# The split of the first columns of x on VectorE and ScalarE, and the later columns' GpSimd operations spread over the feed-forward's blocks

## Chip, cores and metric

The kernel runs on one core of a Trainium2 chip. The metric is device time in microseconds (us) per execution, and the number compared is the median of several. TensorE (PE) does matrix products, VectorE (DVE) and GpSimd (POOL) elementwise work, ScalarE (ACT) elementwise functions, and SyncE's queue (SP) issues all DMAs. Every engine takes its instructions in the order in which they are queued on it.

## What is computed

Attention with queries pooled in pairs, followed by a feed-forward network with g = h - tanh(h). The attention's output, rearranged to 4608 tokens of 512 columns, is the feed-forward's x.

```python
def _attn_ref(q, k, v):                      # (8, 8, 1152, 64) each
    q_pool = q.reshape(B, H, S // 2, 2, D).mean(axis=3)
    scores = (1.0 / np.sqrt(D)) * np.matmul(q_pool, k.transpose(0, 1, 3, 2))
    scores = scores - np.max(scores, axis=-1, keepdims=True)
    attn = np.exp(scores)
    attn = attn / (np.sum(attn, axis=-1, keepdims=True) + 1e-09)
    return np.matmul(attn, v)

def _moe_ref(x, w_in, w_out):                # (4608, 512), (512, 2048), (2048, 512)
    h = x @ w_in
    g = h - np.tanh(h)
    return g @ w_out
```

## The kernel before

**Precision.** Every operand of a large matrix product is split in a high part, rounded to the fp32r format, and a low part, the remainder; a product is the sum of high x high, high x low and low x high. So x exists as `x_h` and `x_l`, each for four feature tiles of 128 (the index `hp`, 0 to 3).

**Attention** runs over 32 pairs of heads (`n_pair`), each in 36 units (`U`). A unit is one key tile of one head and half of the queries: two score matmuls into `ps_s`, one exponential on ScalarE into `p_f`. Each six units are a group, for which POOL adds up the exponentials (`z_part`, two additions), and whose value matmuls (`pv`) come some units later. `z_sums` turns the partial sums into row sums on TensorE, `z_out` copies these to `z_s` on ScalarE, and `store` writes the unnormalised output `o_s` to `x_dram` and the sums to `z_dram`. For each batch the sums are read back (`rec`), inverted and written to `r_dram`, so that the division takes place when the feed-forward loads x.

The order of all this is written out by hand: `add(u, f)` puts a piece of work at unit u, after that unit's score matmuls and exponential, and `add(..., at=first)` ahead of them. `end` is 1152, the unit after the last exponential. All engine handles of this stage (`pe`, `act`, `dve`, `pool`, `sp`) are `InOrder`: what is issued through them stays in this order on its engine. All their instructions appear in the profile under line 37, the helper's.

**x.** `load_x` (lines 96 to 121) prepares up to 512 columns (tokens) of x. For each feature tile, `fetch` issues one DMA for the unnormalised x into `x_f` and, for each of two heads and each batch touched, one for the inverted sums into `x_r`; `work` then runs three POOL operations on 128 partitions: the product `x_f` times `x_r` (the division), the high part (times 1 plus 0, rounded on output), and the low part by subtraction. The pool `xt` has one buffer of `x_f` and one of `x_r`, so that the next feature tile's transfer can start only when these are free again. The first columns, chunk 0, are prepared at the end of attention (lines 416 to 421), feature tile j's fetch at unit end - 14 + 8j and its work 5 units later. Six blocks of weights (four of `wi`, two of `wo`) are loaded at units end - 17 to end - 12 into `spare`, buffers of attention that are free by then (lines 424 to 430).

**Feed-forward.** There are ten chunks of columns: eight of 512 and two of 256. For each chunk the loop over `fc` runs through 16 blocks of the hidden dimension: `hidden` makes twelve matmuls into `ps_h` (line 521), an elementwise chain on ScalarE and VectorE (527 to 537), the high part `g_hi` on ScalarE (538) and the low part `g_lo` on POOL (539); `second`, two blocks behind (`LAG`), multiplies by `wo` (line 546). The other weight blocks are loaded at its beginning (lines 509 to 515) into a pool that takes the place of attention's buffers. The x of chunk ci + 1 is prepared in chunk ci: `load_x` in the program at fc = 2, and at fc = 2 to 5 one feature tile each, fetch and three POOL operations together (lines 571 to 576); `x_h` and `x_l` have two pairs of buffers. `issue_after` keeps this work behind the last SP and POOL instruction of attention and does nothing else. In this stage no `InOrder` is used: a scheduler with its own estimate of times picks, for each engine, among what it takes to be ready, the earlier in the program first, and so sets the order on the engine's queue when the kernel is built.

Of the kernel before, what the change touches and what calls it, by code (L numbers as in the profile page):

```python
# [8 lines left out]
F32 = mybir.dt.float32  # L9
F32R = mybir.dt.float32r  # L10
I32 = mybir.dt.int32
AF = mybir.ActivationFunctionType
ALU = mybir.AluOpType
# [30 lines left out]
def kernel(  # L44
# [17 lines left out]
    nc = tc.nc  # L62
    P = 128
    B, NP, _, _, SQ = q.shape
# [28 lines left out]
    wi_dram = dram.tile([NF, P, 2, NP, P], F32, name="wi_dram")  # L93
    wo_dram = dram.tile([NF, P, 2, DM], F32, name="wo_dram")

    def load_x(tiles, sp, pool, t0, n):

        x_h, x_l = (t.rearrange("p (c n) -> p c n", c=NP) for t in tiles())

        t = {}  # L100

        def fetch(hp):
            x = xt.tile([P, 512], F32, name="x_f")
            r = xt.tile([P, 512], F32, name="x_r")
            t[hp] = x, r
            sp.dma_start(x[:, 0:n], x_dram[hp, :, t0:t0 + n])
            c = t0
            while c < t0 + n:
                b, c1 = divmod(c, SQ)
                m = min(SQ - c1, t0 + n - c)  # L110
                for h in range(2):
                    sp.dma_start(r[h * 64:h * 64 + 64, c - t0:c - t0 + m],
                                 r_dram[b, h, hp:hp + 1, c1:c1 + m].broadcast_to([64, m]))
                c += m

        def work(hp):
            x, r = t[hp]
            pool.tensor_tensor(x[:, 0:n], x[:, 0:n], r[:, 0:n], op=ALU.mult)  # L118
            pool.tensor_scalar(x_h[:, hp, 0:n], x[:, 0:n], 1.0, 0.0, op0=ALU.mult, op1=ALU.add)  # L119
            pool.tensor_tensor(x_l[:, hp, 0:n], x[:, 0:n], x_h[:, hp, 0:n].bitcast(F32), op=ALU.subtract)  # L120
        return x_h, x_l, [(lambda hp=hp: fetch(hp), lambda hp=hp: work(hp)) for hp in range(NP)]

    xp = [ctx.enter_context(tc.tile_pool(name="xp0", bufs=2))]

    def x_tile(i):
        return xp[i].tile([P, NP * 512], F32R, name="x")

    op0 = ctx.enter_context(tc.tile_pool(name="op0", bufs=1))
    xt = ctx.enter_context(tc.tile_pool(name="xt", bufs=1))
    rec = ctx.enter_context(tc.tile_pool(name="rec", bufs=2))  # L130
    chunks = [(t, min(512, NTOK - t)) for t in range(0, NTOK, 512)]
    t, n = chunks.pop()
# [4 lines left out]
    with ExitStack() as actx:  # L137
# [3 lines left out]
        op = actx.enter_context(tc.tile_pool(name="op", bufs=1))  # L141
# [7 lines left out]
        pe, act, dve, pool, sp = (InOrder(tc, e) for e in (nc.tensor, nc.scalar, nc.vector, nc.gpsimd, nc.sync))  # L149
# [23 lines left out]
        at, first = {}, {}  # L173
        end = n_pair * U

        def add(u, f, *args, at=at):
            at.setdefault(u, []).append(lambda: f(*args))
# [29 lines left out]
        def hi_part(pi, c0, c1):  # L207
            w = pairs[pi]
            act.activation(w.hi[:, c0:c1], w.kq[:, c0:c1], AF.Copy)

        def lo_part(pi, c0, c1):
            w = pairs[pi]
            dve.tensor_tensor(w.lo[:, c0:c1], w.kq[:, c0:c1], w.hi[:, c0:c1].bitcast(F32), op=ALU.subtract)
# [143 lines left out]
        def reciprocals(eng, b, t):  # L357

            eng.scalar_tensor_tensor(t[:, 0], t[:, 0], 1e-9, t[:, 1], op0=ALU.add, op1=ALU.add)
            eng.reciprocal(t[:, 0], t[:, 0])  # L360

        def spread(dma, b, t):
            dma.dma_start(r_dram[b].rearrange("h a (x n) -> (h a x) n", n=SQ * NP * 2 // P), t[:, 0])
# [51 lines left out]

        tot = []
        x0 = []
        add(end - 15, lambda: x0.extend(load_x(lambda: (x_tile(0), x_tile(0)), sp, pool, *chunks[0])))
        for j in range(NP):
            for i in range(2):  # L420
                add(end - 14 + 8 * j + 5 * i, lambda i=i, j=j: x0[2][j][i]())


        spare = [t.rearrange("p h n -> p (h n)")[:, i:i + 1024] for t in tt[0] for i in range(0, 3072, 1024)]
# [1 line left out]
        for i, (t, w_dram) in enumerate(((wi, wi_dram), (wi, wi_dram), (wi, wi_dram), (wo, wo_dram), (wi, wi_dram), (wo, wo_dram))):  # L426
            f = len(t)
# [47 lines left out]
        for u in range(end + 60):  # L475
            run(u, first)
            if u < end:
                pi, r = divmod(u, U)
                half, r = divmod(r, U // 2)
                g, r = divmod(r, G)  # L480
                h, j = divmod(r, 3)
# [14 lines left out]
            n, slot = divmod(u - 2 * G + 1, G)  # L496
# [20 lines left out]
    def hidden(x_h, x_l, n, fc):  # L517
        h = ps_h.tile([P, 512], F32, name="ps_h")[:, 0:n]
        mm = [(w, x, c) for w, x in ((0, x_h), (0, x_l), (1, x_h)) for c in range(NP)]
        for j, (w, x, c) in enumerate(mm):  # L520
            nc.tensor.matmul(h, wi[fc][:, w, c], x[:, c, 0:n], start=(j == 0), stop=(j == len(mm) - 1))  # L521

        def t(name, dtype=F32, bufs=2):
            return gp.tile([P, 512], dtype, name=name, bufs=bufs)[:, 0:n]
        u, th, s1, s2, w, m = t("g_u"), t("g_t"), t("g_s1"), t("g_s2"), t("g_w"), t("g_m", bufs=1)
        g_h, g_l = t("g_hi", F32R, LAG + 1), t("g_lo", F32R, LAG + 1)
        nc.scalar.activation(u, h, AF.Square)  # L527
        nc.scalar.activation(th, h, AF.Tanh)
        nc.scalar.activation(s2, u, AF.Square, bias=pc[:, 1:2])  # L529
        nc.scalar.activation(s1, u, AF.Square, bias=pc[:, 0:1])  # L530
        nc.scalar.activation(m, u, AF.Relu, bias=pc[:, 2:3])
        nc.vector.scalar_tensor_tensor(w, u, -P0, h, op0=ALU.add, op1=ALU.mult)  # L532
        nc.vector.tensor_tensor(th, h, th, op=ALU.subtract)  # L533
        nc.vector.scalar_tensor_tensor(w, w, PL, u, op0=ALU.mult, op1=ALU.mult)  # L534
        nc.vector.scalar_tensor_tensor(w, s2, P2, w, op0=ALU.add, op1=ALU.mult)  # L535
        nc.vector.scalar_tensor_tensor(s1, s1, P1, w, op0=ALU.add, op1=ALU.mult)  # L536
        last = nc.vector.copy_predicated(s1, m.bitcast(I32), th).ins  # L537
        nc.scalar.activation(g_h, s1, AF.Copy)  # L538
        nc.gpsimd.tensor_tensor(g_l, s1, g_h.bitcast(F32), op=ALU.subtract)  # L539
        return g_h, g_l, last  # L540

    def second(po, g_h, g_l, _, nt, fc):
        for j in range(nt):
            ts = slice(j * P, (j + 1) * P)
            for i, (g, w) in enumerate(((g_h, 0), (g_h, 1), (g_l, 0))):
                nc.tensor.matmul(po[j], g[:, ts], wo[fc][:, w],  # L546
                                 start=(fc == 0 and i == 0), stop=(fc == NF - 1 and i == 2))

    def store(po, t0, nt, ci):
        if ci == len(chunks) - 1:  # L550
            o_n = x_tile((ci + 1) % 2).bitcast(F32).rearrange("p (j n) -> p j n", n=DM)
        for j in range(nt):
            if ci == len(chunks) - 1:
                o_s = o_n[:, j]
            else:
                o_s = gp.tile([P, DM], F32, name="o_s", bufs=2)
            nc.scalar.activation(o_s, po[j], AF.Copy)
            nc.sync.dma_start(out[t0 + j * P:t0 + (j + 1) * P, :], o_s)

    waiting = []  # L560
    xs = x0
    for ci, (t0, n) in enumerate(chunks):
        x_h, x_l, _ = xs
        po = []
        for fc in range(NF):
            g = hidden(x_h, x_l, n, fc)
            if tot and fc == 3:
                with tc.issue_after(g[2]):
                    reciprocals(nc.vector, *tot[0])
                spread(nc.sync, *tot.pop(0))  # L570
            if fc == 2 and ci + 1 < len(chunks):
                xs = load_x(lambda: (x_tile((ci + 1) % 2), x_tile((ci + 1) % 2)), nc.sync, nc.gpsimd, *chunks[ci + 1])
            if 2 <= fc < 2 + NP and ci + 1 < len(chunks):
                with tc.issue_after(after[0]), tc.issue_after(after[1]):
                    for f in xs[2][fc - 2]:
                        f()

            def rest(po=po, g=g, fc=fc, t0=t0, nt=n // P, ci=ci):
                if fc == 0:
                    po += [ps_o.tile([P, DM], F32, name="ps_o") for _ in range(nt)]  # L580
                second(po, *g, nt, fc)
                if fc == NF - 1:
                    store(po, t0, nt, ci)
            waiting.append(rest)
            if len(waiting) > LAG:
                waiting.pop(0)()
# [36 lines left out]
```

## Time and profile before

| | before |
|---|---|
| median of 3 runs | 1829.13 us (1827.97 to 1831.86) |
| the profiled execution | 1830.94 us, of which its span, first to last instruction, is 1829.2 us |
| granted TensorE clock, mean | 0.992 of full speed |
| TensorE matmul, busy | 1742.4 us (95%) |
| VectorE | 1384.6 us (76%) |
| ScalarE | 1082.5 us (59%) |
| GpSimd | 1063.9 us (58%) |

Attention ends at about 987 us in this trace with the last exponential. The feed-forward's first matmuls stand between attention's last ones, and from 1007 us on TensorE runs the feed-forward alone; its last chunk of 512 columns ends at about 1720 us.

A row of a timeline gives the start in us, the duration, the engine (PEld is TensorE's weight load, SPq the issue of a DMA by SyncE), the line, the operation with output and inputs, the number of merged instructions and, in brackets, how long the engine had been idle and what ended this. A row of a list of waits gives the total in us, how often, and the longest.

### The profile page before, as it was taken

Reading aid. Unit: us, or ns where it says so; the run is one execution under the profiler, and the core shown is the slowest. Engines: PE = TensorE matmul, PEld = TensorE weight load, DVE = VectorE, ACT = ScalarE, POOL = GpSimd, SP = SyncE. Lnnn points to the kernel's source line nnn. Section 1 sums busy time; section 2 is a strip of 40 time slices with the busy share of each in tenths; the row PEclk is TensorE's granted clock in tenths of the full one; section 3 lists DMA queues with packets and bytes.
Section 4 is the critical chain, followed back from the end, with each engine's and each line's share of the span. In section 5 each row is a group of like instructions: output and inputs, shape, how many; then the busy total and the mean of one; then the engine's idle time right before and its main releaser. Section 6 shows DMA issues by size and latency. Waiting matters only on the chain. (4 is left out here: it accounts for less than half of the span.)

```text
span 1829.2 us, 28257 instructions
## 1 busy us (share of the span) xinstructions
PE 1742.4 (95%) x9920; PEld 1308.2 (72%) x9920; DVE 1384.6 (76%) x1815; ACT 1082.5 (59%) x2469; POOL 1063.9 (58%) x768
## 2 busy tenths in 40 slices
PE   4999999999999989999997999999999999999998
PEld 3666666766676666666664767878787888888886
DVE  5876668677667777786740788888889899988897
ACT  2555555656565555555653656666666666666676
POOL 2676678777787767777876375352535344433432
PEclk9999999999999999999998999999999999999999
DMA  7777687878878686878764822020201020101000
GB/s 208 204 181 208 175 220 204 222 199 220 224 209 233 168 213 180 214 210 229 194 167 129 312 54 68 5 66 6 64 7 64 7 63 15 47 12 35 26 18 18
DMA packets 104141, 242.28 MB, mean 132 GB/s; under 512 B 18113, under 2 KB 43329, under 8 KB 104001
## 3 DMA queue, kind: packets, MB, share of 16 engines
q1 hardware_dynamic: 104000, 240.49, 47.8%
q8 instruction: 78, 1.28, 0.3%
q14 instruction: 63, 0.51, 0.1%
HBM read 109.64 MB, written 36.42 MB: 80 GB/s over the span
## 5 line engine op out<-in xcount | busy, mean ns | idle before, releaser
L37 DVE TENSOR_REDUCE mx<-ps_m 128x2 f32<-128x768 f32 x448 | 405.8, 924 | 264.1 <-PE ps_m L37 263.8
L37 ACT ACTIVATE p_f<-ps_s 128x288 f32<-128x288 f32 x1152 | 418.1, 412 | 190.2 <-PE ps_s L37 165.4
L37 PE MATMUL ps_s<-t 128*128 128x288 f32 (+1 forms) x2304 | 447.9, 314 | 14.9 <-ACT p_f L37 8.8
L37 PEld LDWEIGHTS ps_s<-t 128*128 128x128 f32 (+1 forms) x2304 | 357.6, 191 | 119.5 <-issue 90.4
L539 POOL TENSOR_TENSOR g_lo<-g_s,g_hi 128x512 fp32r<-128x512 f32 (+1 forms) x160 | 210.2, 1315 | 394.5 <-ACT g_hi L538 338.7
L37 POOL TENSOR_TENSOR z<-p_f 128x576 f32<-128x576 f32 x192 | 287.7, 1498 | 156.2 <-PE ps_s L37 110.8
L521 PE MATMUL ps_h<-x,wi 128*128 128x512 f32 (+1 forms) x1440 | 326.9, 371 | 0.0
L37 PE MATMUL ps_o<-p_f,v 128*64 128x288 f32 x2304 | 326.0, 419 | 0.0
L37 POOL TENSOR_TENSOR z<-z,p_f 128x576 f32<-128x576 f32 x192 | 290.8, 1515 | 17.7 <-ACT p_f L37 3.0
L521 PEld LDWEIGHTS ps_h<-x,wi 128*128 128x128 f32 x1440 | 255.9, 189 | 52.1
L546 PE MATMUL ps_o<-wo,g_hi 128*128 128x512 f32 x1008 | 274.9, 392 | 3.5 <-ACT g_hi L538 3.4
L37 PE MATMUL ps_m<-x,bd 128*128 128x384 f32 x864 | 238.5, 356 | 32.1 <-DVE mx L37 17.3
L37 PEld LDWEIGHTS ps_o<-p_f,v 128*64 128x64 f32 x2304 | 150.0, 138 | 114.9 <-issue 30.1
L546 PEld LDWEIGHTS ps_o<-wo,g_hi 128*128 128x128 f32 x1008 | 186.8, 188 | 45.5 <-ACT g_hi L538 6.5
L532 DVE SCALAR_TENSOR_TENSOR g_w<-g_u,ps_h 128x512 f32<-128x512 f32 (+1 forms) x160 | 100.4, 628 | 111.6 <-PE ps_h L521 68.8
L527 ACT ACTIVATE g_u<-ps_h 128x512 f32<-128x512 f32 (+1 forms) x160 | 87.8, 549 | 158.2 <-PE ps_h L521 158.1
L37 PEld LDWEIGHTS ps_m<-x,bd 128*128 128x128 f32 x864 | 143.8, 196 | 49.7 <-DVE mx L37 27.1
L546 PE MATMUL ps_o<-wo,g_lo 128*128 128x512 f32 x504 | 159.5, 393 | 6.5 <-POOL g_lo L539 6.3
L538 ACT ACTIVATE g_hi<-g_s 128x512 fp32r<-128x512 f32 (+1 forms) x160 | 94.3, 589 | 119.4 <-DVE g_s L537 117.3
L534 DVE SCALAR_TENSOR_TENSOR g_w<-g_w,g_u 128x512 f32<-128x512 f32 (+1 forms) x160 | 164.6, 1029 | 0.0
L537 DVE COPY_PREDICATED g_s<-g_m,g_t 128x512 f32<-128x512 int32 (+1 forms) x160 | 134.4, 840 | 14.6 <-DVE g_s L536 0.5
L536 DVE SCALAR_TENSOR_TENSOR g_s<-g_s,g_w 128x512 f32<-128x512 f32 (+1 forms) x160 | 126.8, 792 | 17.1 <-DVE g_w L535 0.5
(60 smaller groups left out, 1913.3 us busy)
## 6 DMA issues: line engine op xcount, KB each, us to landing
t<-x SPq DMA_DIRECT2D x64, 432.0 KB
q_n<-in_q_dram SPq DMA_DIRECT2D x32, 576.0 KB
kq<-in_k_dram SPq DMA_DIRECT2D x32, 576.0 KB
t<-kq_l SPq DMA_DIRECT2D x64, 288.0 KB
t<-x SPq DMA_DIRECT2D x64, 288.0 KB
v<-in_v_dram SPq DMA_DIRECT2D x32, 576.0 KB
bd<-x SPq DMA_DIRECT2D x64, 144.0 KB
t<-kq_l SPq DMA_DIRECT2D x64, 144.0 KB
```

The lines of the kernel that those rows point to most:

```text
L37: ins = self.tc.keep_in_program_order(f(*args, **kwargs))
L521: nc.tensor.matmul(h, wi[fc][:, w, c], x[:, c, 0:n], start=(j == 0), stop=(j == len(mm) - 1))
L527: nc.scalar.activation(u, h, AF.Square)
L532: nc.vector.scalar_tensor_tensor(w, u, -P0, h, op0=ALU.add, op1=ALU.mult)
L534: nc.vector.scalar_tensor_tensor(w, w, PL, u, op0=ALU.mult, op1=ALU.mult)
L536: nc.vector.scalar_tensor_tensor(s1, s1, P1, w, op0=ALU.add, op1=ALU.mult)
L537: last = nc.vector.copy_predicated(s1, m.bitcast(I32), th).ins
L538: nc.scalar.activation(g_h, s1, AF.Copy)
L539: nc.gpsimd.tensor_tensor(g_l, s1, g_h.bitcast(F32), op=ALU.subtract)
L546: nc.tensor.matmul(po[j], g[:, ts], wo[fc][:, w], start=(fc == 0 and i == 0), stop=(fc == NF - 1 and i == 2))
```

## The change

`load_x` no longer takes an engine for all of `work`, but one engine for division and low part (`mul`) and a function for the high part (`hi`), and gives back four steps for each feature tile: `fetch`, `divide`, `hi_part`, `lo_part`.

For chunk 0 the division and the low part go to VectorE and the high part to ScalarE (an activation `Copy`), in the written order of these engines. Feature tile j's fetch is at unit end - 18 + 7j, and the three operations 5, 6 and 7 units later.

For the later chunks all three stay on POOL. The program has them one for each `fc`: feature tile hp is fetched at fc = 1 + 3hp, divided at 2 + 3hp, and its parts follow at 3 + 3hp and 4 + 3hp, the last at the same fc as the next tile's fetch.

```diff
-    def load_x(tiles, sp, pool, t0, n):
+    def load_x(tiles, sp, mul, hi, t0, n):
...
-        def work(hp):
+        def divide(hp):
             x, r = t[hp]
-            pool.tensor_tensor(x[:, 0:n], x[:, 0:n], r[:, 0:n], op=ALU.mult)
-            pool.tensor_scalar(x_h[:, hp, 0:n], x[:, 0:n], 1.0, 0.0, op0=ALU.mult, op1=ALU.add)
-            pool.tensor_tensor(x_l[:, hp, 0:n], x[:, 0:n], x_h[:, hp, 0:n].bitcast(F32), op=ALU.subtract)
-        return x_h, x_l, [(lambda hp=hp: fetch(hp), lambda hp=hp: work(hp)) for hp in range(NP)]
+            mul.tensor_tensor(x[:, 0:n], x[:, 0:n], r[:, 0:n], op=ALU.mult)
+
+        def hi_part(hp):
+            hi(x_h[:, hp, 0:n], t[hp][0][:, 0:n])
+
+        def lo_part(hp):
+            mul.tensor_tensor(x_l[:, hp, 0:n], t[hp][0][:, 0:n], x_h[:, hp, 0:n].bitcast(F32), op=ALU.subtract)
+        return x_h, x_l, [[lambda hp=hp, f=f: f(hp) for f in (fetch, divide, hi_part, lo_part)] for hp in range(NP)]
...
-        add(end - 15, lambda: x0.extend(load_x(lambda: (x_tile(0), x_tile(0)), sp, pool, *chunks[0])))
+        add(end - 19, lambda: x0.extend(load_x(lambda: (x_tile(0), x_tile(0)), sp, dve,
+                                               lambda o, x: act.activation(o, x, AF.Copy), *chunks[0])))
         for j in range(NP):
-            for i in range(2):
-                add(end - 14 + 8 * j + 5 * i, lambda i=i, j=j: x0[2][j][i]())
+            for i, x in enumerate((0, 5, 6, 7)):
+                add(end - 18 + 7 * j + x, lambda i=i, j=j: x0[2][j][i]())
...
-            if fc == 2 and ci + 1 < len(chunks):
-                xs = load_x(lambda: (x_tile((ci + 1) % 2), x_tile((ci + 1) % 2)), nc.sync, nc.gpsimd, *chunks[ci + 1])
-            if 2 <= fc < 2 + NP and ci + 1 < len(chunks):
+            if fc == 1 and ci + 1 < len(chunks):
+                xs = load_x(lambda: (x_tile((ci + 1) % 2), x_tile((ci + 1) % 2)), nc.sync, nc.gpsimd,
+                            lambda o, x: nc.gpsimd.tensor_scalar(o, x, 1.0, 0.0, op0=ALU.mult, op1=ALU.add), *chunks[ci + 1])
+            if ci + 1 < len(chunks):
                 with tc.issue_after(after[0]), tc.issue_after(after[1]):
-                    for f in xs[2][fc - 2]:
-                        f()
+                    for i in range(4):
+                        hp, first = divmod(fc - 1 - i, 3)
+                        if first == 0 and 0 <= hp < NP:
+                            xs[2][hp][i]()
```

## The prediction

> **What bounds the kernel now.** I began with the page's table of busy time and the list of what TensorE waited for.
>
> ```profile
> PE 1742.4 (95%) x9920; PEld 1308.2 (72%) x9920; DVE 1384.6 (76%) x1815; ACT 1082.5 (59%) x2469; POOL 1063.9 (58%) x768
> ```
>
> ```profile
> PE ps_o L546 <- POOL g_lo L539: 11.6, 12, 2.1
> PE ps_h L521 <- POOL x L37: 9.9, 3, 5.8
> ```
>
> TensorE is the bound: 95% of the span is matmul. The change touches none of it, so what there is to win is TensorE's idle time behind x. Two waits are of that kind: 9.9 us for x itself, all of it where attention hands over to the feed-forward, and 11.6 us in twelve pieces for `g_lo`, which shares GpSimd (POOL) with the work on x for the later chunks. About 21 us, or 1.2% of the span, is the ceiling of both halves together.
>
> Next the handover, in the timeline (start, duration, engine, line, operation; in brackets the idle time before it):
>
> ```profile
> 971.50 0.41 ACT L37 ACTIVATE z_s<-ps_s 128x288 f32<-128x288 f32 x1 [2.30 <-PE ps_s L37]
> 971.94 0.55 SPq L37 DMA_DIRECT2D z_dram<-z_s  x1
> 972.58 1.34 SPq L37 DMA_DIRECT2D t<-wi_dram  x3
> 973.97 0.42 SPq L37 DMA_DIRECT2D x_f<-x_dram  x1
> ...
> 979.58 2.05 ACT L37 ACTIVATE p_f<-ps_s 128x288 f32<-128x288 f32 x6
> 981.86 1.27 POOL L37 TENSOR_TENSOR x_f<-x_f,x_r 128x512 f32<-128x512 f32 x1 [1.33 <-DMA x_r<-r_dram]
> ...
> 985.23 0.32 SPq L37 DMA_DIRECT2D x_f<-x_dram  x1
> ...
> 985.84 1.44 ACT L37 ACTIVATE p_f<-ps_s 128x288 f32<-128x288 f32 x4 [0.69 <-PE ps_s L37]
> ...
> 989.65 1.27 POOL L37 TENSOR_TENSOR x_f<-x_f,x_r 128x512 f32<-128x512 f32 x1 [1.58 <-DMA x_r<-r_dram]
> ...
> 991.01 0.62 POOL L37 TENSOR_SCALAR x<-x_f 128x512 fp32r<-128x512 f32 x1
> 991.71 1.29 POOL L37 TENSOR_TENSOR x<-x_f,x 128x512 fp32r<-128x512 f32 x1
> 993.02 0.33 SPq L37 DMA_DIRECT2D x_f<-x_dram  x1
> ...
> 996.60 0.41 ACT L37 ACTIVATE z_s<-ps_s 128x288 f32<-128x288 f32 x1 [6.22 <-PE ps_s L37]
> ...
> 1000.81 0.33 SPq L37 DMA_DIRECT2D x_f<-x_dram  x1
> 1002.38 0.58 SPq L37 DMA_DIRECT2D x_dram<-o_s  x1
> 1003.00 0.52 SPq L37 DMA_DIRECT2D z_dram<-z_s  x1
> 1005.72 2.38 SPq L37 DMA_DIRECT2D rec<-z_dram  x4
> 1007.33 9.86 PE L521 MATMUL ps_h<-x,t 128*128 128x512 f32 x36 [5.78 <-POOL x L37]
> ```
>
> The four feature tiles of x pass one at a time, because `x_f` has one buffer: fetch, three POOL operations, and only then the next fetch. From the fetch at 985.23 to the next at 993.02 is 7.79 us: 4.42 us of transfer until the divide starts at 989.65, 3.35 us of POOL to the end of `x_l` at 993.00. The last high part lets TensorE go at 1007.33 after 5.78 us of idle. So the limit here is this serial chain; TensorE has nothing else that may run.
>
> Then what TensorE needs right after those 36 matmuls: `wi[4]`, the first weights that could be loaded only after attention.
>
> ```profile
> 1008.28 1.13 SPq L515 DMA_DIRECT2D wo<-wo_dram  x2
> 1009.46 0.42 SPq L512 DMA_DIRECT2D wi<-wi_dram  x1
> ...
> 1015.34 0.32 SPq L512 DMA_DIRECT2D wi<-wi_dram  x1
> ...
> 1017.02 5.76 PE L521 MATMUL ps_h<-x,wi 128*128 128x512 f32 x24
> ```
>
> The loads stand on SP's queue behind the store of the last softmax sums (1003.00) and its reading back (1005.72). What SP's issues waited for, from the list of waits:
>
> ```profile
> SPq L512 <- DMA wi<-wi_dram: 8.3, 8, 1.7
> ```
>
> So `wi` issues wait for earlier `wi` loads. The issue at 1015.34 is the eleventh of these loads, `wi[4]` the third, and after the first eight or nine SP no longer issues one behind the other but as loads land. So I read 1015.34 as `wi[4]`'s landing. TensorE first uses it at 1017.02: 1.7 us to spare.
>
> **The change at the handover.** Removed: twelve POOL operations. Added: eight VectorE and four ScalarE operations of 128x512, in the fixed order of these engines. Each of the four fetches (one DMA of x, two of r) is queued 4, 5, 6 or 7 units earlier. Prices:
>
> ```profile
> 1016.14 0.68 DVE L534 SCALAR_TENSOR_TENSOR g_w<-g_w,g_u 128x512 f32<-128x512 f32 x1
> 1020.33 0.63 ACT L538 ACTIVATE g_hi<-g_s 128x512 fp32r<-128x512 f32 x1 [0.30 <-DVE g_s L537]
> 1021.04 1.77 POOL L539 TENSOR_TENSOR g_lo<-g_s,g_hi 128x512 fp32r<-128x512 f32 x1 [12.41 <-ACT g_hi L538]
> 1021.76 1.59 DVE L536 SCALAR_TENSOR_TENSOR g_s<-g_s,g_w 128x512 f32<-128x512 f32 x1
> ```
>
> And two rows of the table of stretches (after the engines come the granted clock, the DMA engines' busy share and GB/s):
>
> ```profile
> 984.00:985.00 1.00, 1.00 (x7) 0.91 (x7) 0.00 (x0) 0.90 (x3) 1.00 (x1) 1.00 0.58 221
> 985.00:986.00 1.00, 1.00 (x8) 0.92 (x7) 0.00 (x0) 0.31 (x2) 1.00 (x2) 1.00 0.00 0
> ```
>
> VectorE with two operands in SBUF: 0.68 us alone, 1.59 us for one that fell on a POOL operation. I take 0.68, since VectorE is otherwise empty here (the timeline has no row of it before 1014) and POOL has at most the last two sums left; both ends are kept. High part on ScalarE: 0.63. Some 0.1 us between engines. A tile's work is 0.68 + 0.1 + 0.63 + 0.1 + 0.68 = 2.2 us in place of 3.35.
>
> *Tile 0.* Its fetch is now queued ahead of the three `wi` loads, so it leaves at 972.58 and lands at 977.0 (4.42 us as above; before, behind those loads, it took from 973.97 to 981.8). Its high part stands in ScalarE's order after the exponential of unit end-12, the first of the six at 979.58, hence 979.9 to 980.55; the wait costs nothing, x is there. Low part until 981.35. The three `wi` loads that the fetch is moved past start 1.6 us later; they are wanted only by the first feed-forward matmuls, which need this tile as well.
>
> *Tile 1.* Fetch at 981.4. The row of 984 to 985 shows the engines busy for 0.58 of it and the next row nothing: the six weight loads and tile 0 end at about 984.6, the same bytes whichever goes first. Without a queue tile 1 lands at 985.8. Behind them, with no data moving in the 0.77 us after an issue, as the empty row behind the issue at 985.23 has it, at 984.6 + 3.65 = 988.2. I take 987.5, nearer the queued end, as tile 0 was held up just so. High part 988.3 to 988.95, low part until 989.75. **Here a wait is added**: ScalarE stands at this high part (unit end-5) from about 986 on, and behind it are the last four exponentials, those of 985.84, whose score banks TensorE needs. That pushes the end of attention back by 2 to 3 us, to about 992 for its last matmuls, and costs nothing as long as x is later still, which it is.
>
> *Tiles 2 and 3.* 4.42 + 2.2 us each: fetch 989.8, landed 994.2, done 996.4; fetch 996.45, landed 1000.9, high part done at **1002.3**, with bounds 1000.5 (no queue for tile 1) and 1004.9 (988.2, and two VectorE operations at 1.59). TensorE is freed 5.0 us earlier than 1007.33.
>
> **What is late next.** The copy of the last sums, `z_s`, ran on ScalarE at 996.60, and its store waited only for SP's turn. Now it stands in ScalarE's fixed order behind tile 3's high part (units end+12 and end+9): it can't start before 1002.3. From the start of such a copy to its store is 0.44 us (971.50 to 971.94 for the pair before), so the store goes at 1002.8, just 0.2 us earlier than before, and with it all weight loads. From store to landing of `wi[4]` is 1015.34 - 1003.00 = 12.34 us; it lands at 1015.1. TensorE would come for it at 1002.3 + (1017.02 - 1007.33) = 1012.0. So 3.1 us of the 5.0 turn into a wait for weights, and **1.9 us** stay. With the bounds above it is 3.7 us to -0.7 us.
>
> The same table for one later stretch:
>
> ```profile
> 1009.00:1010.00 1.00, 1.00 (x3) 0.76 (x3) 0.00 (x0) 0.00 (x0) 0.00 (x0) 0.50 0.64 103
> ```
>
> After the idle stretch the granted clock is still 0.50 at 1009 to 1010, which the 36 matmuls pay in both kernels. If the new wait for weights brought on a second such stretch, the 2.7 us from 1007.33 to 1010 at half speed price it at 1.4 us. I keep that as an end of the range and not in the sum, since this row follows a longer idle time (5.78 us) than 3.1.
>
> [...]
>
> **The later chunks.** The same twelve POOL operations per chunk, the same 3 times 4 DMAs on SP, and the same one-buffer chain; only their places in program order move, from the places of fc 2 to 5 to fc 1 to 13. Does the queue follow program order? From the timelines of POOL and TensorE:
>
> ```profile
> 1052.15 1.75 POOL L118 TENSOR_TENSOR x_f<-x_f,x_r 128x512 f32<-128x512 f32 x1
> ...
> 1071.75 1.30 POOL L118 TENSOR_TENSOR x_f<-x_f,x_r 128x512 f32<-128x512 f32 x1 [3.00 <-DMA x_f<-x_dram]
> ...
> 1077.48 1.20 PE L546 MATMUL ps_o<-wo,g_lo 128*128 128x512 f32 x4 [2.06 <-POOL g_lo L539]
> ...
> 1083.62 1.78 POOL L120 TENSOR_TENSOR x<-x_f,x 128x512 fp32r<-128x512 f32 x1
> 1094.13 0.86 PE L521 MATMUL ps_h<-x,t 128*128 128x512 f32 x3
> 1123.48 1.83 POOL L118 TENSOR_TENSOR x_f<-x_f,x_r 128x512 f32<-128x512 f32 x1 [3.28 <-DMA x_r<-r_dram]
> 1184.10 1.07 POOL L119 TENSOR_SCALAR x<-x_f 128x512 fp32r<-128x512 f32 x1 [1.55 <-PE ps_h L521]
> ```
>
> It doesn't. The divide at 1123.48 is of chunk 3's first tile, and its place is in chunk 2, which TensorE reaches after 1184; it ran a good ten fc ahead, as soon as `x_f` was free, and its high part came at 1184.10, when the x buffers were. Since these are not in the fixed order, the scheduler queues each when it takes it to be ready, and a `g_lo` that is ready at that moment stood earlier in the program in both versions. So I expect the same bursts and the same waits: at 1071.75 POOL sat 3.00 us on a transfer, `g_lo` stood behind the two operations that follow, and TensorE lost 2.06 us at 1077.48. I put this half at 0, with bounds from -11.6 (every such wait gone) to the loss in rival C.
>
> **Sum.** -1.9 us. The profiled execution took 1830.94 us, its span 1829.2; both would fall to 1829.0 and 1827.3. On the median of the three times shown, 1829.13, it makes **1827.2 us**.
>
> **Rivals.** A: the weights aren't late, because the loads don't hang on the sums' store (they were only queued after it). Then 5.0 us stay: 1824.1. Against it: SP issued nothing between the fetch at 993.02, with its two r transfers, and the one at 1000.81, and no load was put there. B: one GpSimd operation per fc does hold, `g_lo` is never behind three at once, and two thirds of the 11.6 us go too: 1829.13 - 1.9 - 7.7 = 1819.5. For it: each of those waits follows a burst. Against: the queue that runs ahead. C, the slow side: the order by fc holds in the first chunk, where there is least room. x comes only from 1052.15 on, behind the weight loads; the eleventh operation, tile 3's high part, would stand ten fc of 5.6 us later, at 1108, where TensorE wants it at 1094.8. It decides from a slip of (1094.8 - 1082) / 10 = 1.3 us per operation, tile 3's high part having ended by 1082 (its low part starts at 1083.62). Some 13 us late, less 1.9: up to 1840, more likely near 1836, as second-layer matmuls fill part. D: nothing comes of the change, the first tile's earlier fetch being eaten by the queue of weights and VectorE slowed by POOL: 1829.1.
>
> **How the numbers follow.** Forecast 42% (its own range 1825.4 to 1831.2: -3.7, and +0.7 with 1.4 of clock), A 15%, B 17%, C 14%, D 12%. Faster by over 0.2%, which is 3.7 us and about what a measurement of this kernel can tell, means under 1825.5: all of B, most of A, a few per cent of the forecast: 0.35. Slower, over 1832.8: C and a few per cent of the others: 0.16. Within: 0.49. The range 1818 to 1834 takes in the centres of all but C and leaves out its greater part and B's last few us.
>
> **What would show it.** Right: POOL has only sums between 970 and 1000; the first x fetch stands ahead of the three `wi` loads; TensorE's idle time before the 36 matmuls falls from 5.78 and they start near 1002; `z_s` follows tile 3's high part on ScalarE; then TensorE waits some 3 us for `wi`, a row that the list of waits lacks now. Wrong: no such row (A); `g_lo`'s 11.6 us shrinking (B); TensorE waiting for `x` of line 120 or its neighbours at a chunk's start (C); the four fetches still 7.8 us apart (D).

## The result, and the profile after

| | before | after |
|---|---|---|
| median of 22 runs each, taken side by side | 1830.45 us (1827.53 to 1833.72) | 1826.41 us (1823.6 to 1830.71) |
| ratio, 95% interval | | 0.998 (0.9973 to 0.9987) |
| the profiled execution, its span | 1830.94, 1829.2 us | 1825.99, 1824.2 us |

The change makes the kernel faster by about 3.7 us, between 2.4 and 4.9 (1830.45 times the interval). The lines of the code moved: the first layer's matmul is line 526 now, the second's 551, `g_lo` 544, the weight loads 517 and 520, the three GpSimd operations on x 118, 578 and 124.

The busy time of the engines, and four rows of the list of what TensorE waited for:

```profile
PE 1741.4 (95%) x9920; PEld 1306.6 (72%) x9920; DVE 1403.8 (77%) x1823; ACT 1084.0 (59%) x2473; POOL 1050.4 (58%) x756
```

```profile
PE ps_o L551 <- POOL g_lo L544: 9.8, 14, 1.7
PE ps_h L526 <- ACT x L37: 6.7, 2, 4.7
...
PE ps_h L526 <- DVE g_s L541: 1.4, 1, 1.4
...
PE ps_h L526 <- DMA t<-wi_dram: 0.6, 1, 0.6
```

One more row of the same list, of the kernel before:

```profile
PE ps_s L37 <- POOL z L37: 3.0, 1, 3.0
```

TensorE's work is the same. Its wait for x has gone from 9.9 us to 6.7, the longest piece from 5.8 to 4.7. The 3.0 us that TensorE waited in before for GpSimd's last sum of exponentials, which stood there behind the work on tile 1 (989.65 to 993.00), are gone. The last two rows of after are new: 0.6 us for the first feed-forward weights, whose loads now stand behind the first fetch, and 1.4 us for which the profile names VectorE as the one that came last; the timeline points to something else. Here is the handover in the timeline of the changed kernel:

```profile
969.65 0.41 ACT L37 ACTIVATE z_s<-ps_s 128x288 f32<-128x288 f32 x1 [2.30 <-PE ps_s L37]
...
970.67 0.43 SPq L37 DMA_DIRECT2D x_f<-x_dram  x1
972.33 1.53 SPq L37 DMA_DIRECT2D t<-wi_dram  x3
976.45 1.26 DVE L37 TENSOR_TENSOR x_f<-x_f,x_r 128x512 f32<-128x512 f32 x1 [32.20 <-DMA x_r<-r_dram]
978.00 0.62 ACT L37 ACTIVATE x<-x_f 128x512 fp32r<-128x512 f32 x1
...
986.06 0.79 DVE L37 TENSOR_TENSOR x_f<-x_f,x_r 128x512 f32<-128x512 f32 x1 [6.52 <-DMA x_r<-r_dram]
986.88 0.63 ACT L37 ACTIVATE x<-x_f 128x512 fp32r<-128x512 f32 x1 [1.89 <-DVE x_f L37]
...
987.56 1.75 PE L526 MATMUL ps_h<-x,t 128*128 128x512 f32 x4 [1.98 <-ACT x L37]
988.26 0.33 SPq L37 DMA_DIRECT2D x_f<-x_dram  x1
...
994.68 0.33 SPq L37 DMA_DIRECT2D x_f<-x_dram  x1
996.24 0.58 SPq L37 DMA_DIRECT2D x_dram<-o_s  x1
999.19 0.69 DVE L37 TENSOR_TENSOR x_f<-x_f,x_r 128x512 f32<-128x512 f32 x1 [4.54 <-DMA x_r<-r_dram]
999.91 0.63 ACT L37 ACTIVATE x<-x_f 128x512 fp32r<-128x512 f32 x1 [5.69 <-DVE x_f L37]
1000.45 0.39 ACT L37 ACTIVATE z_s<-ps_s 128x288 f32<-128x288 f32 x1
...
1000.59 10.55 PE L526 MATMUL ps_h<-x,t 128*128 128x512 f32 x36 [4.73 <-ACT x L37]
1000.87 0.52 SPq L37 DMA_DIRECT2D z_dram<-z_s  x1
1002.58 2.38 SPq L37 DMA_DIRECT2D rec<-z_dram  x4
...
1012.20 0.32 SPq L517 DMA_DIRECT2D wi<-wi_dram  x1
...
1012.54 5.84 PE L526 MATMUL ps_h<-x,wi 128*128 128x512 f32 x24 [1.40 <-DVE g_s L541]
```

The reader is to see four things. The first fetch (970.67) now stands ahead of the weight loads (972.33). The feature tiles follow each other at 6.42 us (fetches at 988.26 and 994.68), not 7.79. The copy `z_s` starts at 1000.45, in the very moment in which ScalarE comes out of tile 3's high part; a row of SP's waits shows who held the store back:

```profile
SPq L37 <- ACT z_s L37: 4.0, 1, 4.0
```

And the eleventh weight load is issued at 1012.20, which I read as the landing of `wi[4]`, as before; 0.34 us later TensorE goes on. So I take the new wait for one for weights; in e1 and e7 below, at the same place, the profile itself names a load of weights.

The same stretch in the table of stretches (PE busy share second, granted clock third from the end):

```profile
988.00:991.00 3.00, 3.00 (x12) 1.93 (x12) 0.23 (x1) 0.81 (x3) 2.03 (x2) 0.50 0.53 138
...
999.00:1005.00 6.00, 4.41 (x10) 3.47 (x11) 1.38 (x2) 0.93 (x2) 0.00 (x0) 0.50 0.04 7
...
1012.00:1016.00 4.00, 3.46 (x15) 2.85 (x16) 3.79 (x7) 3.71 (x8) 1.01 (x1) 1.00 1.02 412
```

TensorE runs at half clock from 988 to 991 and from 999 to 1005, each time behind a wait for x (1.98 us ahead of 987.56, 4.73 us ahead of 1000.59), but not behind the 1.4 us at 1012.54.

**Where the time came from.** Single traces of this kernel differ by some us in stages that no edit touches: attention up to the copy of the previous pair's `z_s` took 966.6 to 971.5 us in ten traces of the same instructions. I therefore measure the handover from that copy (971.50 before, 969.65 after) to the first matmul on `wi`, line 521 or 526 (1017.02 and 1012.54). It is 45.52 us before and 42.89 after, a gain of **2.6 us**. For the 55 us from that copy on I also added up, in stretches of a quarter of a microsecond, TensorE's idle time and what half clock cost it (busy time times the missing share of the clock). Idle time fell from 12.9 to 8.7 us, while the loss to the clock rose from 2.6 to 3.9. These are two single traces. Below, e1 repeats the handover of after and takes 43.6 us, e2 that of before and takes 46.6, so each of these times is good to about 1 us. The other 1.1 us of the 3.7 are not explained. The two traces show 0.8 of it in chunk 0, from the first `wi` matmul to the first high part for chunk 2, which waits until chunk 0 has read its own x (76.5 us before, 75.7 after), but that stretch scattered between 73.8 and 77.6 us over the ten traces, so I put nothing on it.

### The profile page after: what moved, and what is told of

It is laid out like the page before. It is cut to its first block, busy times and chain, and to the rows that moved or that the text cites. A ratio compares the mean times of both kernels' runs of the same rounds, so it can differ in the third digit from the quotient of the medians.

```text
span 1824.2 us, 28257 instructions
## 1 busy us (share of the span) xinstructions
PE 1741.4 (95%) x9920; PEld 1306.6 (72%) x9920; DVE 1403.8 (77%) x1823; ACT 1084.0 (59%) x2473; POOL 1050.4 (58%) x756
## 5 line engine op out<-in xcount | busy, mean ns | idle before, releaser
L37 PEld LDWEIGHTS ps_m<-x,bd 128*128 128x128 f32 x864 | 143.5, 196 | 49.6 <-DVE mx L37 27.9
L539 DVE SCALAR_TENSOR_TENSOR g_w<-g_w,g_u 128x512 f32<-128x512 f32 (+1 forms) x160 | 172.6, 1079 | 0.0
L540 DVE SCALAR_TENSOR_TENSOR g_w<-g_s,g_w 128x512 f32<-128x512 f32 (+1 forms) x160 | 129.3, 808 | 18.8 <-ACT g_s L534 2.2
```

The source lines that it names most:

```text
L37: ins = self.tc.keep_in_program_order(f(*args, **kwargs))
```

## The experiments

The first four ran together on one chip with 26 runs of before, the other four on another with 29. The last columns come from their traces: the start of the 36 matmuls, of the store of the last sums, and of the first `wi` matmul, each counted from the copy named above; then TensorE's idle time and loss to the clock in the 55 us from it.

| kernel | ratio to before, 95% | 36 matmuls | store | first `wi` matmul | idle | clock |
|---|---|---|---|---|---|---|
| before | | 35.8 | 31.5 | 45.5 | 12.9 | 2.6 |
| after | 0.998 (0.9973 to 0.9987) | 30.9 | 31.2 | 42.9 | 8.7 | 3.9 |
| e1 first columns only | 0.9975 (0.9965 to 0.9985) | 31.3 | 31.6 | 43.6 | 8.5 | 4.6 |
| e2 later columns only | 0.9993 (0.9982 to 1.0005) | 35.6 | 31.6 | 46.6 | 12.2 | 4.5 |
| e3 sums' copy ahead | 0.997 (0.9958 to 0.9983) | 30.2 | 26.8 | 40.9 | 6.6 | 4.2 |
| e4 two buffers | 0.9946 (0.9931 to 0.996) | 27.8 | 28.3 | 41.5 | 7.8 | 4.9 |
| e5 reading back late | 0.9978 (0.9967 to 0.9989) | 32.3 | 32.6 | 42.9 | 8.6 | 4.2 |
| e6 first fetch behind weights | 0.9992 (0.9982 to 1.0002) | 34.1 | 34.4 | 45.9 | 10.6 | 5.2 |
| e7 e4 and e5 together | 0.9952 (0.9937 to 0.9968) | 27.9 | 28.4 | 36.7 | 4.2 | 1.7 |
| e8 GpSimd at the new units | 1.0016 (1.0004 to 1.0029) | 38.1 | 33.9 | 49.2 | 13.8 | 4.8 |

### e1 and e2: each half of the change alone

e1 takes the change and puts the later chunks' operations back to their old places:

```diff
-            if fc == 1 and ci + 1 < len(chunks):
+            if fc == 2 and ci + 1 < len(chunks):
...
-            if ci + 1 < len(chunks):
+            if 2 <= fc < 2 + NP and ci + 1 < len(chunks):
                 with tc.issue_after(after[0]), tc.issue_after(after[1]):
-                    for i in range(4):
-                        hp, first = divmod(fc - 1 - i, 3)
-                        if first == 0 and 0 <= hp < NP:
-                            xs[2][hp][i]()
+                    for f in xs[2][fc - 2]:
+                        f()
```

> Only the first columns' part of the change; the later chunks' operations stand at fc = 2 to 5 as before. My theory (all of the gain is made at the handover, the queue of GpSimd in the later chunks being set by readiness and not by program order): 3 to 4 us under the kernel before, the same as the whole change within 1 us; from the copy of the previous pair's sums to the first matmul on wi 42.9 us as after the change (45.5 before). Rival (the spread of the later chunks' operations makes a good part of it): 1 to 2 us under the kernel before.

e2 is the other half: chunk 0 on GpSimd at the units of before, the later chunks spread.

```diff
-        add(end - 19, lambda: x0.extend(load_x(lambda: (x_tile(0), x_tile(0)), sp, dve,
-                                               lambda o, x: act.activation(o, x, AF.Copy), *chunks[0])))
+        add(end - 15, lambda: x0.extend(load_x(lambda: (x_tile(0), x_tile(0)), sp, pool,
+                                               lambda o, x: pool.tensor_scalar(o, x, 1.0, 0.0, op0=ALU.mult, op1=ALU.add), *chunks[0])))
         for j in range(NP):
-            for i, x in enumerate((0, 5, 6, 7)):
-                add(end - 18 + 7 * j + x, lambda i=i, j=j: x0[2][j][i]())
+            for i, x in enumerate((0, 5, 5, 5)):
+                add(end - 14 + 8 * j + x, lambda i=i, j=j: x0[2][j][i]())
```

> Only the later chunks' part; the first columns stay on GpSimd at their old units. My theory: no change against the kernel before, within 1 us, and 45.5 us from the copy of the previous pair's sums to the first matmul on wi. Rival: 1 to 2 us faster, and the waits of TensorE for g_lo well under the 11.6 us of before.

e1 alone took 1827.04 us against 1831.85, as much as the whole change gains, and e2 took 1830.46, with an interval that holds no change. TensorE's waits for `g_lo` in e2, and two rows of GpSimd's timeline in it:

```profile
PE ps_o L551 <- POOL g_lo L544: 12.3, 13, 2.0
```

```profile
1124.13 1.29 POOL L118 TENSOR_TENSOR x_f<-x_f,x_r 128x512 f32<-128x512 f32 x1 [3.24 <-DMA x_r<-r_dram]
1184.20 1.07 POOL L578 TENSOR_SCALAR x<-x_f 128x512 fp32r<-128x512 f32 x1 [1.55 <-PE ps_h L526]
```

The wait is 12.3 us with the spread and 11.6 in before. The divide of chunk 3's first tile still runs at 1124 and its high part at 1184, the moment at which the x buffers come free: before has them at 1123.48 and 1184.10. So the places by `fc` do not hold the operations back. From the first `wi` matmul to the end, before takes 812.1 us, e2 811.4 and after 811.6.

### e3: the copy of the last sums ahead of tile 3's high part

```diff
-            for i, x in enumerate((0, 5, 6, 7)):
+            for i, x in enumerate((0, 5, 9, 10) if j == NP - 1 else (0, 5, 6, 7)):
```

> The changed kernel, with tile 3's high and low part three units later (end + 12 and end + 13), so that the copy of the last sums stands ahead of the high part on ScalarE. My theory (the loads of the later weights hang on this copy's store): the store leaves at about 997 instead of 1001 on the changed kernel's clock of events, the weight loads start some 4 us earlier, TensorE's wait of 1.4 us ahead of the first wi matmul is gone, and the time is 1.4 us under that of the change. Rival (the loads hang on something else, and were only queued behind the store): the loads start where they did and the time is the same.

The timeline of e3:

```profile
996.30 0.41 ACT L37 ACTIVATE z_s<-ps_s 128x288 f32<-128x288 f32 x1 [0.65 <-PE ps_s L37]
...
997.57 0.58 SPq L37 DMA_DIRECT2D x_dram<-o_s  x1
998.19 0.52 SPq L37 DMA_DIRECT2D z_dram<-z_s  x1
1000.95 2.38 SPq L37 DMA_DIRECT2D rec<-z_dram  x4
...
1001.66 10.81 PE L526 MATMUL ps_h<-x,t 128*128 128x512 f32 x36 [4.27 <-ACT x L37]
...
1010.98 0.32 SPq L517 DMA_DIRECT2D wi<-wi_dram  x1
...
1012.31 5.76 PE L526 MATMUL ps_h<-x,wi 128*128 128x512 f32 x24
```

The copy and the store no longer wait for the last tile: the store leaves 26.8 us behind the reference copy, not 31.2. `wi[4]` is there at 1010.98, TensorE comes for it at 1012.31 and has no idle time before that row. That the weights hang on the store is shown. What binds now is the 36 matmuls themselves: they start 4.27 us after TensorE ran dry and take 10.81 us. In time e3 is not told apart from the change (0.997 and 0.998, intervals overlapping); in the trace its handover is 2.0 us shorter.

### e4: two buffers for the fetches of chunk 0

`x_f` and `x_r` of chunk 0 come from the two buffers `w_raw`, which are free by then.

```diff
-    def load_x(tiles, sp, mul, hi, t0, n):
+    def load_x(tiles, sp, mul, hi, t0, n, xr=None):
...
+            if xr is None:
...
+            else:
+                x, r = xr()
...
+        def two():
+            raw = wp.tile([P, WB, 2], I32, name="w_raw", bufs=2).rearrange("p n w -> p (n w)").bitcast(F32)
+            return raw[:, 0:512], raw[:, 512:1024]
...
-                                               lambda o, x: act.activation(o, x, AF.Copy), *chunks[0])))
+                                               lambda o, x: act.activation(o, x, AF.Copy), *chunks[0], xr=two)))
```

> The changed kernel with two buffers for x and the inverted sums of the first columns, taken from a pool of attention that is idle by then, so that a feature tile's transfer no longer waits for the low part of the tile before it. My theory (the serial chain of transfer and three operations sets when TensorE goes on): tile 1 lands no earlier, being queued behind the weight loads, tiles 2 and 3 land about 2 and 6 us earlier, tile 3's high part ends 6 us earlier; the store of the last sums then goes about 5 us earlier and with it the weight loads, and 5 us less from the copy of the previous pair's sums to the first wi matmul. Rival (the transfers share a limited rate, so that overlapping them brings nothing): the last tile lands within 2 us of where it did and the time is that of the change.

The timeline of e4 (the first layer's matmul is its line 534):

```profile
995.57 0.41 ACT L37 ACTIVATE o_s<-ps_o 128x288 f32<-128x288 f32 x1 [4.08 <-PE ps_o L37]
995.88 0.62 ACT L37 ACTIVATE x<-w_raw 128x512 fp32r<-128x512 f32 x1
...
997.80 8.47 PE L534 MATMUL ps_h<-x,t 128*128 128x512 f32 x36
...
1011.49 4.57 PE L534 MATMUL ps_h<-x,wi 128*128 128x512 f32 x12 [5.22 <-DMA wo<-wo_dram]
```

Tile 3's high part at 995.88 waits for nothing but its turn behind the copy of `o_s`; x is no longer late, and the 36 matmuls follow attention's without idle time, in 8.47 us. But TensorE then waits 5.22 us for weights: what was a spare 1.7 us in before is now the longest wait of the handover. And it has a price behind it, in the table of stretches of e4:

```profile
1010.00:1011.00 1.00, 0.00 (x0) 0.00 (x0) 0.88 (x2) 1.00 (x3) 0.92 (x1) 1.00 1.02 410
...
1012.00:1014.00 2.00, 2.00 (x6) 1.56 (x5) 2.00 (x4) 1.20 (x2) 0.00 (x0) 0.50 1.02 416
```

The clock is 1.00 while TensorE still waits, and 0.50 from about 1011.5 on. The handover is 1.4 us shorter than with the change, not 5: tile 3's high part ends only 4.4 us earlier (26.5 us behind the reference copy), and the copy of the last sums then waits for attention's own matmuls, so that the store leaves 2.9 us earlier. Even so e4 is the fastest of the first four in time: 1823.13 against 1831.85, about 9.9 us better than before and some 6 better than the change. Its trace shows 6.8 us of that up to chunk 1; the rest, at the edge of the interval (7.3 to 12.6), I can't place.

### e5 and e7: the reading back of the last sums moved behind the weight loads

e5 is the change with the last batch's `sums` issued inside the loop over weights, after eight blocks; e7 is e4 with the same edit.

```diff
-                if w.hp == NP - 1:
+                if w.hp == NP - 1 and w.b < B - 1:
                     add(u + 6, lambda: tot.append((w.b, sums(w.b))))
...
+        if f == 8:
+            tot.append((B - 1, sums(B - 1)))
+            after = sp.last, after[1]
```

> The changed kernel, with the reading back of the last batch's sums put on SP's queue behind the first ten of the late weight loads instead of ahead of them; its results are wanted only by the eighth chunk. My theory (the late weights are held by what stands ahead of them on SP's queue, the store of the last sums and this reading back): the loads start 2.5 to 4 us earlier, TensorE's wait of 1.4 us for the first of them is gone, and the time from the copy of the previous pair's sums to the first wi matmul falls from 43 to about 41.5 us, 1 to 1.5 us under the change in all. Rival (the loads wait for attention's buffers to be free, which the reading back has no part in): they start at the same time, and nothing changes.

> Two buffers for the first columns' x and the late reading back together. My theory (with two buffers TensorE stood 5.2 us waiting for the late weights): the loads start 2.5 to 4 us earlier than with two buffers alone, TensorE's wait falls from 5.2 to between 1 and 2.7 us, and the time is 2.5 to 4 us under two buffers alone, about 12 us under the kernel before. Rival: as with two buffers alone.

The timelines of e5 and of e7:

```profile
1001.46 0.52 SPq L37 DMA_DIRECT2D z_dram<-z_s  x1
1003.31 0.80 SPq L520 DMA_DIRECT2D wo<-wo_dram  x2
```

```profile
999.79 0.52 SPq L37 DMA_DIRECT2D z_dram<-z_s  x1
1001.76 0.80 SPq L528 DMA_DIRECT2D wo<-wo_dram  x2
...
1008.07 5.84 PE L537 MATMUL ps_h<-x,wi 128*128 128x512 f32 x24 [0.34 <-DMA wi<-wi_dram]
```

The loads start 1.85 us after the store in e5 and 1.97 in e7, against 4.27 in after (1000.87 to 1005.14). So 2.4 us of the delay was the reading back. The rest is close to the 1.71 us that lie between the store and the reading back in after, so I take it for the landing of the store; whether a load needs it, because the pool of weights takes the place of attention's buffers, `z_s` among them, is not shown. In e5 the wait for weights is gone, but the handover is no shorter: tile 1 happened to land 1.2 us later, everything behind it followed, and the 36 matmuls took 10.81 us. As a test of time e5 is inconclusive (1826.49 us, ratio as the change's). In e7 the 5.22 us of idle time shrink to 0.34 and the second slow stretch is not there: 36.7 us of handover, 8.8 less than before. Yet of that the trace of e4 had made good 3 us in chunk 0 (73.8 us from the first `wi` matmul to the first high part for chunk 2, against 76.7 in e7), and in time e7, at 1822.6 us beside 1830.62 of before, is not told apart from e4 (ratios 0.9952 and 0.9946). e4 and e7 both beat the two kernels of the study.

### e6: the first fetch behind the weight loads again

```diff
-            for i, x in enumerate((0, 5, 6, 7)):
+            for i, x in enumerate((4, 5, 6, 7) if j == 0 else (0, 5, 6, 7)):
```

> The changed kernel with tile 0's transfer put back behind the three wi loads on SP's queue (unit end - 14), all else as in the change. My theory (half of tile 0's time was the queue, but tile 1 is held by the same weight loads anyway): tile 0 lands 3 to 4 us later, ScalarE stands at its high part for some 2 us with exponentials behind it, tile 1 lands 0 to 2 us later, and tile 3's high part 0.5 to 2 us later; 0 to 1.5 us slower than the change, the wait for weights taking up a part. Rival (the early transfer is the main part of the gain): 2.5 us or more slower than the change, as slow as before.

The timeline of e6, and a row of its stretches:

```profile
979.29 0.69 DVE L37 TENSOR_TENSOR x_f<-x_f,x_r 128x512 f32<-128x512 f32 x1 [35.71 <-DMA x_r<-r_dram]
980.02 0.63 ACT L37 ACTIVATE x<-x_f 128x512 fp32r<-128x512 f32 x1 [2.57 <-DMA t<-wo_dram]
...
980.70 1.65 PE L526 MATMUL ps_h<-x,t 128*128 128x512 f32 x3 [2.66 <-ACT x L37]
...
989.13 0.63 ACT L37 ACTIVATE x<-x_f 128x512 fp32r<-128x512 f32 x1
```

```profile
981.00:986.00 5.00, 5.00 (x19) 2.92 (x18) 0.67 (x2) 1.37 (x4) 0.00 (x0) 0.50 0.56 192
```

The loss is the rival's and not the 0 to 1.5 us of my theory: e6 is as slow as before within its interval, some 2 us above the change, and 3.0 us in the handover. Tile 0 is divided 10.3 us behind the reference copy, not 6.8. Tile 1's divide starts at 985.71, 16.7 us behind that copy, nearly as in after (16.4), so little was lost in the transfers. But ScalarE had stood 2.57 us at tile 0's high part with exponentials queued behind it, and TensorE 2.66 us, after which it ran at half clock to almost 987. Tile 1's high part, behind those late exponentials, came only 3.4 us after the start of its divide (989.13), where in after it follows in 0.8 (986.06 to 986.88). The delay is carried through to the 36 matmuls (34.1 against 30.9). It is the fixed order of two engines, and the clock behind it, that made the late tile expensive here.

### e8: GpSimd at the new units

```diff
-        add(end - 19, lambda: x0.extend(load_x(lambda: (x_tile(0), x_tile(0)), sp, dve,
-                                               lambda o, x: act.activation(o, x, AF.Copy), *chunks[0])))
+        add(end - 19, lambda: x0.extend(load_x(lambda: (x_tile(0), x_tile(0)), sp, pool,
+                                               lambda o, x: pool.tensor_scalar(o, x, 1.0, 0.0, op0=ALU.mult, op1=ALU.add), *chunks[0])))
```

> The changed kernel, with the first columns' three operations back on GpSimd, at the change's new units: the earlier transfers without the change of engine. My theory (the chain is shortened by both, 1.1 us per tile by the faster engines and some 2 us in all by the earlier start): the period from one transfer to the next is again 7.8 us for the later tiles, tile 3's high part ends 2 to 4 us later than with the change, but the copy of the last sums no longer waits for it; 1 to 3 us under the kernel before and 1 to 2.5 us over the change. Rival (the change of engine does it all): as the kernel before.

GpSimd's timeline in e8, and the fetch that follows on SP:

```profile
976.78 1.27 POOL L37 TENSOR_TENSOR x_f<-x_f,x_r 128x512 f32<-128x512 f32 x1 [1.73 <-DMA x_r<-r_dram]
...
978.73 1.43 POOL L37 TENSOR_TENSOR z<-p_f 128x576 f32<-128x576 f32 x1
980.23 1.40 POOL L37 TENSOR_TENSOR z<-z,p_f 128x576 f32<-128x576 f32 x1
981.59 1.27 POOL L37 TENSOR_TENSOR x<-x_f,x 128x512 fp32r<-128x512 f32 x1
982.89 0.32 SPq L37 DMA_DIRECT2D x_f<-x_dram  x1
```

With the steps at three separate units, the sums of exponentials come in between on GpSimd's fixed order: tile 0 takes from 976.78 to 982.86, 6.1 us for 3.2 us of work, and the next fetch waits for the end of it. Tile 1 fares the same way, and the handover is 3.6 us longer than in before. My theory, 1 to 3 us under before, was wrong: the medians are 1833.43 and 1830.62 us. So the earlier places, with the three steps apart, lose on GpSimd; on VectorE nothing comes in between. Earlier places on GpSimd with the three steps together, as in before, were not run, so how much of the gain is the change of engine alone stays open.

## Why the prediction was right, and where its size was off

The forecast was 1829.13 - 1.9 us; measured are -3.7 (-2.4 to -4.9), -2.6 of it shown in the handover. The mechanism is the one forecast. Its gain was put too low, by 0.7 us in the handover of the traces and by 1.8 in the medians, and the 1.1 us between these two are not explained. By the time alone rival A, at -5.0, is even a little nearer than the forecast; it is the traces that decide between them. That 1826.41 us lies so close to the forecast 1827.2 is in part luck: the three runs it started from had a median of 1829.13, the 22 of before have 1830.45. In the table below the predicted times are counted from 971.50 and the measured from 969.65.

| step | predicted | measured |
|---|---|---|
| tile 0 lands | 5.5 | 6.8 |
| its high part starts | 8.4 | 8.35 |
| tile 1 is fetched, lands | 9.9, 16.0 | 9.9, 16.4 |
| tile 2 is fetched | 18.3 | 18.6 |
| tile 3 is fetched | 24.95 | 25.0 |
| tile 3's high part ends | 30.8 | 30.9 |
| the store of the sums leaves | 31.3 | 31.2 |
| TensorE is through with the 36 matmuls | 40.5 | 41.5 |
| first `wi` matmul | 43.6 | 42.9 |

**x earlier: right.** A tile's 2.2 us on two engines in place of 3.35, the fetch ahead of the weights, and the half-queued landing of tile 1 gave tile 3's high part to 0.1 us. That it came so close is in part luck: tile 1 landed 0.4 us later than I had taken, and tile 2, with 6.42 us from its fetch to the next and not 6.65, made up for most of it. Tile 0 landed 1.3 us later than priced, which was hidden, as the prediction said, behind the exponential that stands ahead of its high part. The exponential hid a second error too: GpSimd had the sums of three groups left, six additions from 975.76 to 991.78, and not at most two, and the divide of tile 0 took 1.26 us, not 0.68. e6 shows that this cover is thin. Two waits had no term in the sum. The 3.0 us for GpSimd's last sum belong to the idle time behind the work on x in before, which makes the ceiling about 24 us and not 21; and the three `wi` loads that the fetch was moved past did cost TensorE something, 0.6 us at 979.99. Neither moved the end of the handover, which tile 3 and then the weights set.

**`z_s` behind tile 3's high part: right.** The copy starts as that part ends, the store is only 0.3 us earlier than before (0.2 predicted), and e3 shows that it is this order, and with it the store, on which the weights hang. This is what rival A denied.

**The mis-sized term: from the store to `wi[4]`.** I took 12.34 us from before. It was 11.33 (1000.87 to 1012.20). All of the difference lies between the store and the first reading back, which waits for the store to land (2.1 us before and 1.1 after in the list of SP's waits): 2.72 us before (1003.00 to 1005.72), 1.71 after; from there to `wi[4]` both take 9.62. In before, the large store of `o_s` had been issued 0.62 us ahead of the small one, in after 4.63. The eight traces with this pair of issues divide cleanly: 2.53, 2.69, 2.72 and 2.76 us where the large store was 0.62 us ahead, 1.71 to 1.72 where it was at least 2.3. But tile 3's fetch divides them in the same way: in the first four it was issued 2.2 us ahead of the small store and was still under way, in the others it had landed before (in after it was divided at 999.19). Which of the two transfers held the store back, if either did, is not shown. The difference is 1.0 us. Against this 1.0 stands 0.34 us between the eleventh issue and the matmul, which I had left out; 0.7 remains, the difference between 1.9 and 2.6.

**The wait for weights: right in kind, 1.4 us and not 3.1.** 0.7 of that is the landing above, 1.0 is that TensorE came later: chiefly because its 36 matmuls ran at half clock for 4.4 us from their start (to 1005.0), not for 3.0 as in before (1007.3 to 1010.3). That cost nothing, since the weights weren't there. The priced second slow stretch didn't come: the granted clock is 1.00 from 1012 to 1016.

**The later chunks at zero: right.** e2 shows that half to do nothing, which ends rival B, and no slip by `fc` is to be seen, which ends rival C. Rival D falls with the 6.42 us between fetches. One sentence was right only for this kernel: that pushing attention's last matmuls back costs nothing while x is later still. They went back by more than the 2 to 3 us forecast: the value matmuls end 24.0 us behind the copy, 18.4 before. In e4 x is not later, and those matmuls then set the start of the 36.

## What to carry to other kernels

When work is moved into an engine's fixed order, list what stands behind it there and who waits for that: here the copy of a few sums, a store, its landing, a reading back and then all the weights. Moving to an idle engine paid where earlier places on the busy one, with the steps apart, lost, and a second buffer (e4) was worth more than either. A wait that comes after another has been shortened is priced with the queue as it will be, not as it was: from the small store to its reading back it was 2.72 us in before and 1.71 in after.

## What the runs showed of the hardware

**Around the handover the granted clock stood at 0.50 for 3.4 us or a multiple of it.** Read from the granted clock in stretches of half a microsecond, with the mixed ones divided, the times at half clock last 3.4 us (after, e7), 6.8 (after, e6), 13.7 (before), 17.1 (e2) and 20.5 (e8): one, two, four, five and six times 3.41. Waits of 1.98 to 2.07 us were each followed by such a time (3.4 us in after, e1 and e3, 6.8 in e4), waits of 1.17 to 1.40 (e1, after, e6) by none. In attention waits of 1.39 us (before, ahead of 197.81), 1.60 (before, 674.23) and 1.62 (after, 672.42) each had 3.4 us at 0.50 behind them. So the length of the one wait does not decide alone, and what does is not shown. No run here keeps TensorE busy through the waits. Part of the scatter between runs goes with the clock: of the 29 runs of before beside e5 to e8, the ten with a mean clock of 0.991 or less have a median of 1832.1 us, the 13 with 0.993 or more one of 1828.6.

**A VectorE operation with two operands in SBUF took 0.69 us where GpSimd was idle** (after, 999.19) and 0.79 to 1.26 where GpSimd worked beside it (after, 986.06 and 976.45), up to 1.93 in e4 (988.89). In these three GpSimd's addition had begun first. Where VectorE began first, at 977.51 in e3, it took 0.69 us, and the addition that GpSimd began 0.05 us later took 1.92 in place of 1.41.

**Steady blocks took three paces in the trace of before.** At a granted clock of 1.00 throughout, one block of 24 matmuls of the feed-forward took 5.10, 5.44 or 5.54 us at different times of one and the same execution, the first and the last in the same chunk (before: 1404.72, 1143.16 and 1440.59, from one `g_lo` to the next). What decides is open. By my estimate ten blocks at 5.44 us in place of 5.10 make 3.4 us, which is why the handover was compared by itself.
